# Chunk attention with a Mish FFN on Trainium2: softmax tiles transposed side by side, one more pair by DMA, q and k asked for earlier

## The chip, the cores and the metric

One core of one Trainium2 chip. The metric is the device time of one execution in microseconds; of several runs the median is taken. The kernel before takes 796.45 us (median of three runs, 796.07 to 797.13).

## What is computed

Attention within chunks of 64 tokens, then a feed-forward layer with the Mish function, all in float32:

```python
scores = scale * np.matmul(q_c, k_c.transpose(0, 1, 2, 4, 3))
scores = scores - np.max(scores, axis=-1, keepdims=True)
attn = np.exp(scores)
attn = attn / (np.sum(attn, axis=-1, keepdims=True) + 1e-09)
out = np.matmul(attn, v_c)
...
h = x @ w_in
sp = np.where(h > 20.0, h, np.log1p(np.exp(np.minimum(h, 20.0))))
g = h * np.tanh(sp)
return (g @ w_out).astype(np.float32)
```

q, k and v have 8 batches, 8 heads, 576 tokens and 64 columns; x has 4608 rows of 512, w_in is 512 by 2048, w_out 2048 by 512.

## The kernel before, in words

**Tiles and pairs.** The 4608 tokens are 36 tiles of 128; attention works on 18 pairs of tiles. The first eight tiles go through the FFN in a plain phase (lines L389 and L424), in which the attention of the first eight pairs (0 to 7) is done as well. The other 28 tiles form four blocks of 896 rows.

**The Strassen phase.** For the four blocks both FFN products are done by a Strassen scheme with seven products in place of eight. Each block has eight sets of 14 steps, 32 sets in all. An even step is one up product (`s_up`, L881, six matmuls into the banks `al`, `b` or `g`), an odd step one down product (`s_down`, L1000, six matmuls into a bank `d`, one of two that take turns). After a down product `s_out` brings the bank into `totals`, which lies in the room `sums`: by a copy on ACT (L1026) where a block's total is written for the first time, by an addition on DVE (L1028) otherwise. When a block is done, DVE transposes the totals (L1031), and `s_store` (L1044) writes half of them to the output by four DMAs of 224 KB. A block's first copy into a half of `sums` has to wait until the stores of the block before have read that half. The stores of the first block are at steps 137 and 141, those of the second at 249 and 253. The down products run 15 steps behind the up products, so the last eight or so of a block come in the next block's first sets.

**Pairs 8 to 17** are worked in beside the steps. `MEET` lists the steps at which the pairs meet: pair 8 has its scores at step 36 and its values at step 50, where the scores of pair 9 follow, and so on. `plan_pair` (L1235) puts each operation of a pair at a step: q and k are asked for 9 steps ahead of the scores (`p_load`, L707), v three steps after them (`load_v`, L246), then come max, subtraction (DVE), exponential (ACT), sum and normalisation (`p_norm`, L760, DVE). The normalised tile has to be transposed before the values are formed. Pairs with 14 or 19 steps between scores and values do that on the PE (`p_transpose`, L770, eight matmuls with the identity into `pt`, and two copies on ACT, L778). The pairs with 28 or 56 steps (pairs 10, 11, 13, 15, 16) do it by DMA: POOL splits the words of a tile into two halves of 16 bits (`p_split`, L787), a DMA on SyncE's queue transposes them (`p_turn`, L793), and POOL joins them (`p_join`, L799).

**Places.** Room `c` has three places of 2 KB per partition. Tiles 0 and 1 of a pair lie in places 0 and 1; tile 0 is split into place 2, transferred back into place 0 and joined into place 2. Tile 1 is split into place 0, so its split comes after tile 0's join, seven steps later. The room `x32` has 14 KB for the rows of the next block and 2 KB (`waits`, at 14 KB) in which one tile of pair 7 and one of pair 14 waits until `x_late` (L696, steps 44 and 240). q, k and v of the pairs share three buffers of the pool `at`, together with a sum `xs` at steps 98, 210 and 322.

**The order of the work** is written out by hand. In each step `s_set` issues the up or the down product (and with it the load of the next ring tile, L861, after every fourth up product, and of a wo tile, L866, after every second down product), then the PE's operations of the pairs, then `s_out`, then the list of operations that are due at this step. Each engine, and SyncE's queue of DMAs, works in that order; an instruction that waits holds those behind it on its engine. The ring loads (1024 KB) are issued two ring tiles ahead, the wo loads (512 KB) three products ahead.

Of the kernel before, what the change touches and what calls it, by code (L numbers as in the profile page):

```python
# [13 lines left out]
U16 = mybir.dt.uint16  # L14
# [4 lines left out]
P = 128  # L19
CHUNK = 64  # L20
# [5 lines left out]
def kernel(  # L26
# [19 lines left out]
    NF, _, DM = w_out.shape  # L46
# [11 lines left out]
    NG = H // 2  # L58
# [16 lines left out]
    KB = 1024  # L75
# [16 lines left out]
    def view(name, start, shape, dtype=F32):  # L92

        n = math.prod(shape)
        o = rooms[name]
        assert start % 4 == 0 and start // 4 + n <= o.shape[1]
        o = o[:, start // 4 : start // 4 + n]
        if dtype != F32:
            o = o.bitcast(dtype)
        if len(shape) > 1:  # L100
            names = "abcde"[: len(shape)]
            o = o.rearrange(
                f"p ({' '.join(names)}) -> p {' '.join(names)}", **dict(zip(names, shape))
            )
        return o
# [123 lines left out]
    st = {}  # L229
# [13 lines left out]
    def load_v(j, vs=None):  # L243
        if vs is None:
            vs = at.tile([P, 2, H, D], F32, name=f"v_{j}", tag="A")
        nc.sync.dma_start(out=vs, in_=v[2 * j : 2 * j + 2].rearrange("t p h c -> p t h c"))  # L246
        st[j]["v"] = vs
# [429 lines left out]
    x32 = []  # L677
# [20 lines left out]
    def a_x(j, t):  # L698
        x_put(2 * j + t, st[j]["av", 0][:, :, t])
# [4 lines left out]
    def p_load(j):  # L704
        qk = [at.tile([P, 2, H, CHUNK], F32, name=f"{n}_{j}", tag="A") for n in "qk"]
        for x, src in zip(qk, (q, k)):
            nc.sync.dma_start(out=x, in_=src[2 * j : 2 * j + 2].rearrange("t p h c -> p t h c"))  # L707
        st[j] = {"q": qk[0], "k": qk[1]}

    def p_scores(j, z):  # L710
        d = st[j]
        o = places["a", z - 1], places["b"]
        for c in range(2):
            d["s", c] = o[c].rearrange("p (t g k) -> p t g k", t=2, g=NG)
        for t in range(2):
            for g in range(NG):
                for h in range(2):
                    for c in range(2):
                        rows = slice(c * CHUNK, (c + 1) * CHUNK)
                        nc.tensor.matmul(  # L720
                            d["s", c][h * CHUNK : (h + 1) * CHUNK, t, g],
                            lhsT=d["q"][rows, t, 2 * g + h],
                            rhs=d["k"][rows, t, 2 * g + h],
                            start=True,
                            stop=True,
                        )

    def p_max(j, c):
        st[j]["m", c] = m = sm_p.tile([P, 2, NG], F32, name=f"m_{j}_{c}", tag="m")
        nc.vector.tensor_reduce(out=m, in_=st[j]["s", c], op=ALU.max, axis=AX.X)  # L730

    def p_sub(j, c):
        d = st[j]
        if c == 0:
            d["pp"] = view("c", 0, [2, NG, 2, CHUNK])
            for t in range(2):
                d["p", t] = d["pp"][:, t]
        nc.vector.tensor_tensor(
            out=d["pp"][:, :, :, c],
            in0=d["s", c],  # L740
            in1=d["m", c].unsqueeze(3).broadcast_to([P, 2, NG, CHUNK]),
            op=ALU.subtract,
        )

    def p_exp(j, t):
        p = st[j]["p", t]
        nc.scalar.activation(out=p, in_=p, func=AF.Exp, scale=SCALE)

    def p_sum(j, t):
        r = small(j, "r", slice(t, t + 1))  # L750
        nc.vector.tensor_reduce(
            out=r.rearrange("p c n -> p n c"), in_=st[j]["p", t], op=ALU.add, axis=AX.X
        )
        nc.vector.tensor_scalar(out=r, in0=r, scalar1=1e-9, scalar2=None, op0=ALU.add)
        nc.vector.reciprocal(out=r, in_=r)

    def p_norm(j, t):
        p = st[j]["p", t].rearrange("p g c k -> p c g k")
        r = st[j]["r", t]
        nc.vector.tensor_tensor(  # L760
            out=p, in0=p, in1=r.unsqueeze(3).broadcast_to([P, 2, NG, CHUNK]), op=ALU.mult
        )

    def p_transpose(j):
        d = st[j]
        pool, tag = home[0]
        d["pt"] = pool.tile([P, 2, NG, P], F32, name=f"pt_{j}", tag=tag)
        for t in range(2):
            for g in range(NG):
                nc.tensor.transpose(  # L770
                    out=d["pt"][:, t, g],
                    in_=d["p", t][:, g].rearrange("p c k -> p (c k)"),
                    identity=ident,
                )

    def p_copy(j, t):
        d = st[j]
        nc.scalar.copy(  # L778
            out=d["p", t].rearrange("p g c k -> p (g c k)"),
            in_=d["pt"][:, t].rearrange("p g n -> p (g n)"),  # L780
        )

    def half_words(slot):
        return view("c", 2 * KB * slot, [DM]).bitcast(U16)

    def p_split(j, t):
        nc.gpsimd.tensor_copy(  # L787
            out=half_words((2, 0)[t]).rearrange("p (b n) -> p b n", b=2),
            in_=half_words(t).rearrange("p (n b) -> p b n", b=2),
        )  # L790

    def p_turn(j, t):
        nc.sync.dma_start_transpose(  # L793
            out=half_words(t).rearrange("p (m n) -> p m n", n=P), in_=half_words((2, 0)[t])
        )

    def p_join(j, t):
        st[j]["p", t] = view("c", 2 * KB * (2, 0)[t], [NG, 2, CHUNK])
        nc.gpsimd.tensor_copy(  # L799
            out=half_words((2, 0)[t]).rearrange("p (n b) -> p b n", b=2),  # L800
            in_=half_words(t).rearrange("p (b n) -> p b n", b=2),
        )

    def p_values(j):
        d = st[j]
        o = banks(j, "av", BOTH, home[0])
        for t in range(2):
            ps = d["p", t].rearrange("p g c k -> p (g c) k").unsqueeze(1)
            small_mm(o[:, :, t : t + 1], d["v"][:, t : t + 1], ps, FIRST)
# [377 lines left out]
    def when(z, i, *ops):  # L1187
        due.setdefault((z, i), []).extend(ops)
# [37 lines left out]
        for k, m in (2, 0), (5, 3), (3, 4), (4, 7):  # L1226
            when(z, m, lambda k=k: x_sum(b, k))

    MEET = (36, 50, 64, 92, 148, 162, 190, 204, 260, 288, 307)
    NEAR = dict(exp=5, sum=(6, 7), norm=(7, 8), t=11)  # L1230
    MID = dict(exp=5, sum=(8, 9), norm=(10, 12), t=16)
    FAR = dict(exp=33, sum=(36, 37), norm=(38, 40), t=44)
    pe = {}

    def plan_pair(j, start, end):  # L1235

        n = NEAR if end - start < 16 else MID if end - start < 30 else FAR

        def at_(m, *ops):
            when(*divmod(m, STEPS), *ops)  # L1240

        def on_pe(m, op):
            pe.setdefault(divmod(m, STEPS), []).append(op)

        at_(8 if start == MEET[0] else start - 9, lambda: p_load(j))
        on_pe(start, lambda: p_scores(j, start // STEPS))
        at_(start + 3, lambda: load_v(j))
        for t in range(2):
            at_(start + 1 + 2 * t, lambda t=t: p_max(j, t))
            at_(start + 2 + 2 * t, lambda t=t: p_sub(j, t))  # L1250
            at_(start + n["exp"], lambda t=t: p_exp(j, t))
            at_(start + n["sum"][t], lambda t=t: p_sum(j, t))
            at_(start + n["norm"][t], lambda t=t: p_norm(j, t))
            if end - start < 28:
                at_(start + n["t"] + 1, lambda t=t: p_copy(j, t))
            else:
                m = start + n["norm"][0] + 7 * t
                at_(m + 1, lambda t=t: p_split(j, t))
                at_(m + 2, lambda t=t: p_turn(j, t))
                at_(m + 8, lambda t=t: p_join(j, t))  # L1260
            at_(end + 1, lambda t=t: a_x(j, t))
        if end - start < 28:
            on_pe(start + n["t"], lambda: p_transpose(j))
        on_pe(end, lambda: p_values(j))

# [20 lines left out]
    with tc.manual_schedule():  # L1286
# [38 lines left out]
        for n in "b", "g":  # L1325
            places[n] = ps_b.tile([P, DM], F32, name=n, tag=n)
        for j, pair in zip(range(AHEAD[-1] + 1, NPAIR), zip(MEET, MEET[1:])):
            plan_pair(j, *pair)
# [55 lines left out]
```

## Time and profile before

| what | value |
|---|---|
| median of 3 runs | 796.45 us |
| profiled execution | 795.96 us, span 794.1 us |
| PE busy | 781.3 us (98%) |
| DVE, ACT, POOL busy | 592.6, 475.9, 296.1 us |
| DMA | 204.95 MB, mean 258 GB/s |
| TensorE clock granted | 0.999 of full speed |

The span runs from the first to the last recorded instruction; the time has some 2 us around it. PE is TensorE's matmul, PEld its weight loads, DVE VectorE, ACT ScalarE, POOL GpSimd, SPq the queue of SyncE, from which nearly all DMAs are issued. In rows of the timeline and of the chain the first number is the start and the second the length, in microseconds; "[1.96 <-PE d L1000]" is the idle time of the engine just before and what ended it. "d<-u,wo" names the output and the inputs. Where an instruction waits for several things, the row names the one that came last by the profile.

### The profile page before, as it was taken

Reading aid. Unit: us, or ns where it says so; the run is one execution under the profiler, and the core shown is the slowest. Engines: PE = TensorE matmul, PEld = TensorE weight load, DVE = VectorE, ACT = ScalarE, POOL = GpSimd, SP = SyncE. Lnnn points to the kernel's source line nnn. Section 1 sums busy time; section 2 is a strip of 40 time slices with the busy share of each in tenths; the row PEclk is TensorE's granted clock in tenths of the full one; section 3 lists DMA queues with packets and bytes.
Section 4 is the critical chain, followed back from the end, with each engine's and each line's share of the span. In section 5 each row is a group of like instructions: output and inputs, shape, how many; then the busy total and the mean of one; then the engine's idle time right before and its main releaser. Section 6 shows DMA issues by size and latency. Waiting matters only on the chain.

```text
span 794.1 us, 15299 instructions
## 1 busy us (share of the span) xinstructions
PE 781.3 (98%) x5940; PEld 701.4 (88%) x5940; DVE 592.6 (75%) x929; ACT 475.9 (60%) x855; POOL 296.1 (37%) x259
## 2 busy tenths in 40 slices
PE   8999999999999999999999999999999999999996
PEld 7887888888889999999899999999999999999986
DVE  6897978888866776799577679977575897455666
ACT  5988865666676665555566466647465654644440
POOL 2000026556363235533434435454433452333340
PEclk9999999999999999999999999999999999999999
DMA  7798867989978777765987866689965667866537
GB/s 292 245 312 292 276 229 242 350 285 333 374 244 295 268 263 222 291 225 181 328 333 237 297 254 233 220 234 373 284 235 185 227 217 242 291 224 220 182 117 172
DMA packets 95112, 204.95 MB, mean 258 GB/s; under 512 B 24128, under 2 KB 47168, under 8 KB 87872
## 3 DMA queue, kind: packets, MB, share of 16 engines
q1 hardware_dynamic: 90752, 202.01, 74.9%
q10 hardware_dynamic: 4288, 1.97, 1.0%
q8 instruction: 47, 0.77, 0.4%
q14 instruction: 25, 0.20, 0.1%
HBM read 162.53 MB, written 38.80 MB: 254 GB/s over the span
## 4 chain that ended last, share of the span: by engine, by line
PE 75%; DVE 10%; ACT 6%; DMA 3%; issue 2%; POOL 1%; SPq 0%; DVEq 0%; POOLq 0%; ACTq 0%
PE d L1000 28%; PE al L881 16%; PE o_o L424 8%; PE g L881 8%; PE h L389 7%; PE b L881 4%; DMA k<-in_k 2%; PE av L256 2%; DVE sums L1028 1%; DVE sums L1031 1%; PE al L720 1%; DMA v<-in_v 1%; DVE c L192 1%; PE s L256 1%; DVE c L760 1%
## 5 line engine op out<-in xcount | busy, mean ns | idle before, releaser
L1000 PE MATMUL d<-u,wo 128*128 128x448 f32 x796 | 203.8, 363 | 0.0
L1028 DVE TENSOR_TENSOR sums<-d,sums 128x448 f32<-128x448 f32 x192 | 118.8, 619 | 78.4 <-PE d L1000 78.1
L881 PE MATMUL al<-xo,ring 128*128 128x448 f32 x768 | 174.6, 362 | 0.0
L1000 PEld LDWEIGHTS d<-u,wo 128*128 128x128 f32 x796 | 148.6, 187 | 11.7 <-DVE u L960 0.6
L881 PEld LDWEIGHTS al<-xo,ring 128*128 128x128 f32 x768 | 143.3, 187 | 11.0 <-ACT sums L926 0.5
L881 PE MATMUL g<-xo,ring 128*128 128x448 f32 x384 | 87.6, 363 | 0.2 <-ACT y L926 0.2
L881 PEld LDWEIGHTS g<-xo,ring 128*128 128x128 f32 x384 | 71.6, 187 | 5.4 <-ACT y L926 0.6
L1000 PE MATMUL d<-yr,wo 128*128 128x448 f32 x192 | 56.7, 363 | 0.0
L1000 PE MATMUL d<-xo,wo 128*128 128x448 f32 x182 | 54.9, 364 | 0.0
L1000 PE MATMUL d<-g,wo 128*128 128x448 f32 x174 | 51.9, 363 | 0.2 <-DVE sums L1028 0.2
L950 ACT ACTIVATE b<-b 128x448 f32<-128x448 f32 x32 | 16.9, 528 | 52.0 <-DVE b L936 51.9
L640 POOL TENSOR_TENSOR c<-c 128x256 f32<-128x256 f32 x12 | 10.8, 901 | 98.2 <-DVE c L608 96.2
L881 PE MATMUL b<-xo,ring 128*128 128x448 f32 x192 | 43.6, 362 | 0.0
L950 ACT ACTIVATE y<-y 128x448 f32<-128x448 f32 x22 | 12.7, 577 | 47.6 <-DVE y L936 47.6
L982 POOL TENSOR_TENSOR z<-y,z 128x448 f32<-128x448 f32 x24 | 27.8, 1157 | 35.8 <-DVE y L982 21.9
L424 PE MATMUL o_o<-xo,g 128*128 128x512 f32 x168 | 40.8, 392 | 0.1
L389 PE MATMUL h<-x,xo 128*128 128x512 f32 x168 | 40.9, 392 | 0.0
L950 ACT ACTIVATE z<-g 128x448 f32<-128x448 f32 x32 | 17.4, 544 | 39.0 <-DVE g L936 28.0
L1000 PEld LDWEIGHTS d<-yr,wo 128*128 128x128 f32 x192 | 36.0, 187 | 2.7 <-ACT sums L1026 0.3
L881 PEld LDWEIGHTS b<-xo,ring 128*128 128x128 f32 x192 | 36.0, 187 | 2.5
L424 PEld LDWEIGHTS o_o<-xo,g 128*128 128x128 f32 x168 | 31.2, 188 | 6.6 <-DVE g L411 0.2
L389 PEld LDWEIGHTS h<-x,xo 128*128 128x128 f32 x168 | 31.2, 188 | 6.5
(261 smaller groups left out, 1656.3 us busy)
## 6 DMA issues: line engine op xcount, KB each, us to landing
ring<-dwi SPq DMA_DIRECT2D x56, 1024.0 KB, 7.1
wo<-dwo SPq DMA_DIRECT2D x112, 512.0 KB, 4.5
sums<-in_w_in SPq DMA_DIRECT2D x16, 512.0 KB, 5.4
sums<-in_w_out SPq DMA_DIRECT2D x16, 512.0 KB, 5.6
q<-in_q SPq DMA_DIRECT2D x16, 512.0 KB, 6.4
k<-in_k SPq DMA_DIRECT2D x16, 512.0 KB, 6.9
v<-in_v SPq DMA_DIRECT2D x16, 512.0 KB, 6.3
dwo<-sums SPq DMA_DIRECT2D x15, 512.0 KB, 5.2
```

Of the source, the lines that this page charges most:

```text
L192: nc.vector.scalar_tensor_tensor(out=c, in0=c, scalar=3, in1=a[:, :, 0], op0=left, op1=either)
L256: nc.tensor.matmul(o[h * CHUNK : (h + 1) * CHUNK, c, t - ts.start, g], lhsT=l[rows, t, 2 * g + h], rhs=r[rows, t, 2 * g + h], start=True, ...
L389: nc.tensor.matmul(h[:, cols], lhsT=wi(f, w_, kt), rhs=x[:, kt, cols], start=(n == 0), stop=(n == 3 * NK - 1),)
L424: nc.tensor.matmul(acc[t], lhsT=g[:, sl], rhs=w_part(f, w_), start=(f == 0 and n == 0), stop=(f == NF - 1 and n == 2),)
L640: nc.gpsimd.tensor_tensor(out=o, in0=a, in1=b, op=op)
L720: nc.tensor.matmul(d["s", c][h * CHUNK : (h + 1) * CHUNK, t, g], lhsT=d["q"][rows, t, 2 * g + h], rhs=d["k"][rows, t, 2 * g + h], start=Tr ...
L760: nc.vector.tensor_tensor(out=p, in0=p, in1=r.unsqueeze(3).broadcast_to([P, 2, NG, CHUNK]), op=ALU.mult)
L881: nc.tensor.matmul(o[:, :HALF], lhsT=w_[:, wn, kt * P : (kt + 1) * P], rhs=x[:, xn, kt], start=(n == 0 and k < 3), stop=(n == 5), skip_gro ...
L950: nc.scalar.activation(out=take(z, 12) if n == 12 else i, in_=i, func=AF.Mish)
L982: engine.tensor_tensor(out=o, in0=l, in1=r, op=ALU.subtract)
L1000: nc.tensor.matmul(o[:, :HALF], lhsT=wos[(len(DOWN) * y + kk) % 4][:, i, part, h * P : (h + 1) * P], rhs=x, start=(m == 0 and k in (5, 2, 1)),
L1028: nc.vector.tensor_tensor(out=o, in0=i, in1=o, op=ALU.add)
```

## The change

Three things are altered.

1. A fourth place of 2 KB, the `waits` area of `x32`, joins the three of room `c`. Tile 0 is split into and joined in place 2 as before, tile 1 in place 3. Tile 1's split comes one step after its own normalisation, its transfer one step later, and both joins ten steps after the normalisation (tile 0's was eight). In a pair with 28 steps that puts the splits at steps 11 and 13, the transfers at 12 and 14 and the joins at 20 and 22 after the scores; before they were at 11 and 18, 12 and 19, 18 and 25. In a pair with 56 steps they move from 39, 40, 46 and 46, 47, 53 to 39, 40, 48 and 41, 42, 50.
2. The last pair (17) has its values at step 316, not 307. With 28 steps it is now one of the pairs that go by DMA, the sixth of ten.
3. q and k are asked for 12 steps ahead of the scores, not 9 (the first of the ten pairs, at step 8, is left as it is).

```diff
+    def p_place(n):
+        return ("c", 2 * KB * n) if n < 3 else ("x32", 14 * KB)
+
+    def half_words(n):
+        return view(*p_place(n), [DM]).bitcast(U16)
 
     def p_split(j, t):
         nc.gpsimd.tensor_copy(
-            out=half_words((2, 0)[t]).rearrange("p (b n) -> p b n", b=2),
+            out=half_words(t + 2).rearrange("p (b n) -> p b n", b=2),
             in_=half_words(t).rearrange("p (n b) -> p b n", b=2),
         )
 
     def p_turn(j, t):
         nc.sync.dma_start_transpose(
-            out=half_words(t).rearrange("p (m n) -> p m n", n=P), in_=half_words((2, 0)[t])
+            out=half_words(t).rearrange("p (m n) -> p m n", n=P), in_=half_words(t + 2)
         )
 
     def p_join(j, t):
-        st[j]["p", t] = view("c", 2 * KB * (2, 0)[t], [NG, 2, CHUNK])
+        st[j]["p", t] = view(*p_place(t + 2), [NG, 2, CHUNK])
         nc.gpsimd.tensor_copy(
-            out=half_words((2, 0)[t]).rearrange("p (n b) -> p b n", b=2),
+            out=half_words(t + 2).rearrange("p (n b) -> p b n", b=2),
             in_=half_words(t).rearrange("p (b n) -> p b n", b=2),
         )
...
-    MEET = (36, 50, 64, 92, 148, 162, 190, 204, 260, 288, 307)
+    MEET = (36, 50, 64, 92, 148, 162, 190, 204, 260, 288, 316)
     NEAR = dict(exp=5, sum=(6, 7), norm=(7, 8), t=11)
-    MID = dict(exp=5, sum=(8, 9), norm=(10, 12), t=16)
-    FAR = dict(exp=33, sum=(36, 37), norm=(38, 40), t=44)
+    MID = dict(exp=5, sum=(8, 9), norm=(10, 12))
+    FAR = dict(exp=33, sum=(36, 37), norm=(38, 40))
...
-        at_(8 if start == MEET[0] else start - 9, lambda: p_load(j))
+        at_(8 if start == MEET[0] else start - 12, lambda: p_load(j))
...
-            if end - start < 28:
+            if n is NEAR:
                 at_(start + n["t"] + 1, lambda t=t: p_copy(j, t))
             else:
-                m = start + n["norm"][0] + 7 * t
+                m = start + n["norm"][t]
                 at_(m + 1, lambda t=t: p_split(j, t))
                 at_(m + 2, lambda t=t: p_turn(j, t))
-                at_(m + 8, lambda t=t: p_join(j, t))
+                at_(m + 10, lambda t=t: p_join(j, t))
             at_(end + 1, lambda t=t: a_x(j, t))
-        if end - start < 28:
+        if n is NEAR:
             on_pe(start + n["t"], lambda: p_transpose(j))
         on_pe(end, lambda: p_values(j))
```

## Rows read from the trace of the kernel before

**Rows 1.** The page, busy us, share of the span and instructions by engine.
```profile
PE 781.3 (98%) x5940; PEld 701.4 (88%) x5940; DVE 592.6 (75%) x929; ACT 475.9 (60%) x855; POOL 296.1 (37%) x259
```

**Rows 2.** Waits of PE (columns: us in total, times, longest us).
```profile
PE al L720 <- DMA k<-in_k: 1.0, 2, 0.8
```

**Rows 3.** The chain that ended last around step 304 (start us, us, what).
```profile
594.04 1.20 PE g L881 x6
595.24 0.87 PE pt L770 x8
596.12 1.20 PE d L1000 x6
```

**Rows 4.** Timeline of ACT and of PE's weight loads at two block ends.
```profile
386.91 0.53 ACT L1026 COPY sums<-d 128x448 f32<-128x448 f32 x1 [1.96 <-PE d L1000]
387.74 0.19 PEld L1000 LDWEIGHTS d<-xo,wo 128*128 128x128 f32 x1
534.21 0.53 ACT L1026 COPY sums<-d 128x448 f32<-128x448 f32 x1 [2.47 <-DMA out<-sums]
534.80 0.19 PEld L1000 LDWEIGHTS d<-yr,wo 128*128 128x128 f32 x1 [0.28 <-ACT sums L1026]
```

**Rows 5.** Timeline of SyncE's queue at the two block ends.
```profile
379.92 3.53 SPq L1044 DMA_DIRECT2D out<-sums  x4
384.46 1.36 SPq L793 DMA_TRANSPOSE c<-c  x1
385.87 0.63 SPq L707 DMA_DIRECT2D q<-in_q  x1
526.71 3.65 SPq L1044 DMA_DIRECT2D out<-sums  x4
532.79 0.66 SPq L707 DMA_DIRECT2D q<-in_q  x1
```

**Rows 6.** Single DMA issues at the first block end, with their time to landing.
```profile
L866 SPq DMA_DIRECT2D wo<-dwo x1: 525/525/525, 375.6 to 375.6; - x1
DMA to landing us min/median/max: 3.8/3.8/3.8
L861 SPq DMA_DIRECT2D ring<-dwi x1: 423/423/423, 376.2 to 376.2; - x1
DMA to landing us min/median/max: 5.7/5.7/5.7
L866 SPq DMA_DIRECT2D wo<-dwo x1: 319/319/319, 377.3 to 377.3; - x1
DMA to landing us min/median/max: 5.9/5.9/5.9
L1044 SPq DMA_DIRECT2D out<-sums x1: 1804/1804/1804, 381.6 to 381.6; - x1
DMA to landing us min/median/max: 5.2/5.2/5.2
```

**Rows 7.** Stretches of 2 us: busy by engine, PEclk, DMA share, GB/s.
```profile
376.00:378.00 2.00, 2.00 (x12) 1.81 (x12) 1.97 (x4) 0.97 (x2) 0.00 (x0) 1.00 0.76 172
378.00:380.00 2.00, 2.00 (x12) 1.87 (x11) 1.97 (x5) 1.15 (x3) 1.16 (x1) 1.00 1.06 428
380.00:382.00 2.00, 2.00 (x12) 1.87 (x11) 1.97 (x4) 1.57 (x4) 1.52 (x2) 1.00 0.96 389
526.00:528.00 2.00, 2.00 (x12) 1.88 (x11) 1.93 (x5) 1.34 (x4) 0.93 (x2) 1.00 0.98 403
```

**Rows 8.** DVE's second norm of pair 11, POOL after it, splits and joins.
```profile
374.03 0.67 DVE L760 TENSOR_TENSOR c<-c,r 128x512 f32<-128x512 f32 x1
378.25 1.16 POOL L960 TENSOR_TENSOR u<-sums,yr 128x448 fp32r<-128x448 f32 x1 [4.77 <-ACT yr L954]
L787 POOL COPY c<-c x10: 1037/1040/1262, 301.2 to 564.8; 128x1024 uint16<-128x1024 uint16 x10
L799 POOL COPY c<-c x10: 1343/1352/1757, 310.0 to 569.9; 128x1024 uint16<-128x1024 uint16 x10
```

More of the change, by code (lines that the diff above doesn't have):

```diff
@@ L781, in p_copy @@
         )
-    def half_words(slot):
-        return view("c", 2 * KB * slot, [DM]).bitcast(U16)
+    def p_place(n):
+        return ("c", 2 * KB * n) if n < 3 else ("x32", 14 * KB)
+    def half_words(n):
+        return view(*p_place(n), [DM]).bitcast(U16)
     def p_split(j, t):
         nc.gpsimd.tensor_copy(
-            out=half_words((2, 0)[t]).rearrange("p (b n) -> p b n", b=2),
+            out=half_words(t + 2).rearrange("p (b n) -> p b n", b=2),
             in_=half_words(t).rearrange("p (n b) -> p b n", b=2),
```

## The prediction

> **What bounds the kernel now.** I read the page's busy times first, then the waits of the PE, then the chain that ended last, and only then the queue of SyncE around the places where the change moves something. The PE is busy for 98% of the span [rows 1]. So a microsecond counts only if it is PE work removed, PE idle time removed, or PE idle time added. In the Strassen phase a step (six matmuls) takes 1.20 us [rows 3]; all step numbers below are turned into time by that.
>
> The longest waits of the PE in this phase are two, both for a late k [rows 2]. They belong to pairs 12 and 16, whose scores are due at steps 148 and 260. SyncE shows why: q and k are planned for steps 139 and 251, and there they stand behind four output stores and a transfer by transposition, so they are issued only at 385.87 and 532.79 [rows 5].
>
> One more near-wait decides this case. Steps 137 and 249 each store half of a finished block (four DMAs of 224 KB from `sums`). The next block's first result is copied by ACT into the same half of `sums`, so that copy must wait until all four stores have read it. After the second block ACT sat idle for 2.47 us for those stores, and the PE's next `d` matmul began right when the copy was done [rows 4]. After the first block the last store lands at 381.6 + 5.2 = 386.8 [rows 6] and the copy starts at 386.91; the PE's weight load that needs the freed bank comes at 387.74, 0.3 us after the copy's end at 387.44 [rows 4]. So at both block ends the landing of the stores sets the PE, with 0.3 us to spare in the first and nothing in the second.
>
> **The change part by part.** *The last pair goes by transfer.* Eight transposes leave the PE: the chain shows 0.87 us for them between two full steps [rows 3], so −0.9. The values stand alone on the PE at step 316 as they did at 307, at the same price. Two ACT copies from PSUM go, two splits and two joins come on POOL: 2 × 1.04 + 2 × 1.35 = 4.8 us [rows 8], spread over 11 steps (13 us) on an engine that is 37% busy [rows 1]. I cost that at nothing; without the cover a late join would hold the values at step 316, one for one. Its two transposing DMAs and the later copies into x32 end at step 317, five steps (6 us) before the first reader at 322: nothing.
>
> *Both tiles beside each other.* Tile 1's split no longer waits for tile 0's join: split at norm + 1, transfer one step later. For pair 11 the second norm ends at 374.70 and POOL has nothing from 373.5 on [rows 8], so its split would end near 375.8 and its transfer would be issued right behind the ring load of 376.2 [rows 6], not at 384.46 [rows 5]. Joins now end six steps ahead of the values instead of three, and POOL's subtraction in step 13 no longer queues behind a join and a split. No PE wait of size hangs on either [rows 2]: nothing. If a late split held SyncE there, the loads behind it would wait; the first of them are the wo loads, which are issued three products (12 steps, 14 us) ahead of their use.
>
> *q and k 12 steps ahead.* Slots: three buffers; at steps 136 and 248 one holds v, two are free, so the loads need not wait. In the pairs 14 steps apart they now come one step before the previous pair's v, which has 11 steps (13 us) and so stays hidden. For pairs 12 and 16 k lands long before the scores: the waits of 0.8 and 0.2 go, −1.0 [rows 2].
>
> But what do they overtake? Step 136 and step 248 lie *before* the stores of 137 and 249. In before SyncE issued ring, wo, four stores, transfer, q, k; after, it issues ring, transfer, q, k, wo, four stores. All but the transfer run on the one queue of SyncE. The landings of this queue come in order of issue: wo of 375.6 at 379.4, ring of 376.2 at 381.9, wo of 377.3 at 383.2, last store at 386.8 [rows 6]. And the DMA engines are full in that stretch, with shares of 1.06 and 0.96 (0.98 after the second block) [rows 7]. So 1,049 KB in front push the stores back by the time these bytes take, called D. Nearest rows: the same 1,049 KB of the ring load added 381.9 − 379.4 = 2.5 us [rows 6]; at the 389 to 428 GB/s of this stretch [rows 7] it is 2.5 to 2.7. I take 2.6. Bounds: 0, if the stores are not held by what is in front; 5.7, the ring load's whole time from issue to landing [rows 6], if nothing overlaps. The transfer moving ahead could add up to a microsecond of sharing (hence 3.6 as a practical upper end).
>
> What the PE then loses: D − 0.3 = 2.3 at the first block end, D = 2.6 at the second, 4.9 together. Third block end: no pair is near it, unchanged.
>
> The Trainium skill (DMA: Bandwidth & Descriptors, "Where 436 GB/s comes from") puts loads from HBM at about 358 GB/s for one core; as an estimate from that page, 1,049 KB would take 2.9 us and the sum would be +3.6. The rows of this stretch show more than that, and they are used.
>
> *Sum:* −0.9 − 1.0 + 4.9 = **+3.0 us**. The profiled execution took 795.96 us (span 794.1); the median is 796.45, 0.49 above it. I put the sum on the median: 799.4.
>
> **The rivals.** *A, other side: the stores are not held.* Place: SyncE's queue at 380 and 527 us. If the stores' packets are served beside q and k, D is 0 and only the gains stay: 796.45 − 1.9 = 794.6, faster. It decides at D = 1.1, where 2D − 0.3 equals 1.9. For it: k arrives with time to spare in any case, and stores are small in bytes. Against it: the landings in issue order [rows 6] and full engines [rows 7].
>
> The Trainium skill (DMA: Bandwidth & Descriptors, "Queues, rings and completion order") says that data descriptors carry no barrier, a later one may finish before an earlier one, and completion is not first-in-first-out per issuing engine. By that rule this rival would hold; in the four landings of this case none overtook another, so I give it 0.26 and not more.
>
> *B: D is about half,* since q and k are issued at some 378 to 379 and part of them flows before the stores are ready at 379.92 [rows 5], or because the stores' own four transfers, and not the bytes in front, set their landing. D near 1.1 gives 2.2 − 0.3 − 1.9 = 0: 796.5, within 0.2%. For it: the DMA moved only 172 GB/s in 376 to 378 [rows 7]. Against: that is before q and k can be issued. Chance 0.19.
>
> *C: POOL becomes the limit in the last pair,* a late join holding the values: at most the 1.76 us that a join took beside other work [rows 8], 1.8 − 1.9 and no stores held: also near 796.4. Small, inside B's chance.
>
> **How the numbers follow.** 0.2% of 796.45 is 1.6 us, about what a measurement here can tell from no change. Slower by more needs D above 1.9; faster by more needs D below about 0.3. Forecast (D from 1.9 up): 0.55, at 799.4, its own range 798.0 to 801.5 (D 1.9 to 3.6). B: 0.19. A: 0.26. The range has to reach A, so 794.4 to 801.2; left out are the fast tail of A (gains over 2.1, perhaps 0.1) and D over 3.5 (0.07).
>
> **What would show it.** In the profile of after: no `pt` matmuls from pair 17 (32 instead of 40 of that line) and a step 304 without the 0.87 gap; no wait of the PE for k; q and k issued near 378 and 525 ahead of four stores. Right, if the `d` line shows PE idle of over 2 us near 388 and 535 behind ACT's copy into `sums`, itself waiting for the stores, and these land near 389.4 and 536.7. Wrong, if the copy starts near 387 and 534 as before: then the time is near 794.6 and the failed step is D. New waits of the PE for a join on POOL would make C right.

## The result and the profile after

The changed kernel takes 804.02 us (median of 4 runs, 802.31 to 804.64) against 796.26 us for the kernel before in the same comparison; the ratio is 1.0097, with a 95% interval of 1.0073 to 1.0122. It is slower, as forecast, but by 7.8 us where 3.0 were forecast, and 804.02 lies outside the range. The profiled execution has a span of 802.8 us, 8.7 more than before.

The page's busy line of after, which answers to [rows 1]:

```profile
PE 783.5 (98%) x5932; PEld 703.7 (88%) x5932; DVE 590.4 (74%) x929; ACT 474.6 (59%) x853; POOL 303.3 (38%) x263
```

The PE's busy time hardly moves. The list of its waits on other engines (columns: us in total, times, longest us) has no k any more [rows 2], and a new first line:

```profile
PE d L1003 <- ACT sums L1029: 7.1, 2, 3.6
```

Lines have moved by three: L1026 is L1029 now, L1044 is L1047, L1000 is L1003. The timelines of ACT and of the PE at both block ends, to be held against [rows 4]:

```profile
390.85 0.53 ACT L1029 COPY sums<-d 128x448 f32<-128x448 f32 x1 [6.15 <-DMA out<-sums]
542.59 0.53 ACT L1029 COPY sums<-d 128x448 f32<-128x448 f32 x1 [6.33 <-DMA out<-sums]
```

```profile
386.49 1.36 PE L884 MATMUL g<-xo,ring 128*128 128x448 f32 x6
391.44 0.74 PE L1003 MATMUL d<-xo,wo 128*128 128x448 f32 x1 [3.58 <-ACT sums L1029]
...
399.76 1.36 PE L884 MATMUL g<-xo,ring 128*128 128x448 f32 x6
...
538.28 1.36 PE L884 MATMUL g<-xo,ring 128*128 128x448 f32 x6
543.17 0.47 PE L1003 MATMUL d<-yr,wo 128*128 128x448 f32 x1 [3.53 <-ACT sums L1029]
...
550.68 1.36 PE L884 MATMUL g<-xo,ring 128*128 128x448 f32 x6
```

The same products in the kernel before:

```profile
386.74 1.36 PE L881 MATMUL g<-xo,ring 128*128 128x448 f32 x6
394.79 1.36 PE L881 MATMUL g<-xo,ring 128*128 128x448 f32 x6
533.53 1.36 PE L881 MATMUL g<-xo,ring 128*128 128x448 f32 x6
541.24 1.36 PE L881 MATMUL g<-xo,ring 128*128 128x448 f32 x6
```

From one `g` product to the next it is 399.76 − 386.49 = 13.27 us and 550.68 − 538.28 = 12.40 us. In the kernel before the same two stretches take 8.05 us and 7.71 us. So the block ends lose 5.2 + 4.7 = 9.9 us. Elsewhere the changed kernel gains 1.2 us: 0.25 ahead of the first block end, 0.2 between the two, and 0.7 after the second, where the eight transposes are gone. What is left is the 8.7 us of the span.

Why the copy is late stands in SyncE's queue and in the landings. The row with `c<-x` is the transposing DMA of tile 1, called the second transfer below; that of tile 0, the first transfer, is issued at 373.26, ahead of the rows shown. The issues at the first block end, against [rows 5]:

```profile
376.59 1.77 SPq L796 DMA_TRANSPOSE c<-x  x1
378.41 0.62 SPq L707 DMA_DIRECT2D q<-in_q  x1
379.08 0.57 SPq L707 DMA_DIRECT2D k<-in_k  x1
379.75 0.64 SPq L869 DMA_DIRECT2D wo<-dwo  x1
380.49 4.02 SPq L1047 DMA_DIRECT2D out<-sums  x4
```

Two single issues with their time to landing, against [rows 6]:

```profile
L707 SPq DMA_DIRECT2D k<-in_k x1: 571/571/571, 379.1 to 379.1; - x1
DMA to landing us min/median/max: 7.2/7.2/7.2
L1047 SPq DMA_DIRECT2D out<-sums x1: 1458/1458/1458, 383.1 to 383.1; - x1
DMA to landing us min/median/max: 7.6/7.6/7.6
```

k lands at 379.1 + 7.2 = 386.3, the last store at 383.1 + 7.6 = 390.7, and the copy starts at 390.85. Before, the last store landed at 386.8. The transfers share the queue of the other DMAs, as the page's section on queues shows: the changed kernel has two more transfers of 256 KB, and they are added to q1 (packets, MB, share; first before, then after):

```profile
q1 hardware_dynamic: 90752, 202.01, 74.9%
q1 hardware_dynamic: 92864, 202.53, 75.5%
```

And there is a second loss, which the waits don't list. Stretches of 2 us (columns as in [rows 7]):

```profile
386.00:388.00 2.00, 1.85 (x10) 1.40 (x8) 0.00 (x0) 0.00 (x0) 0.55 (x1) 1.00 1.07 368
388.00:390.00 2.00, 0.00 (x0) 0.00 (x0) 0.00 (x0) 0.00 (x0) 0.00 (x0) 0.98 1.35 312
390.00:392.00 2.00, 0.56 (x2) 0.52 (x3) 0.00 (x0) 1.15 (x3) 0.07 (x1) 0.50 0.78 265
392.00:394.00 2.00, 2.00 (x7) 1.78 (x6) 0.00 (x0) 2.00 (x6) 1.07 (x1) 0.50 1.13 336
394.00:396.00 2.00, 2.00 (x7) 1.50 (x5) 1.16 (x2) 0.92 (x3) 0.00 (x0) 0.50 1.04 299
396.00:398.00 2.00, 2.00 (x105) 1.79 (x108) 0.63 (x1) 0.58 (x1) 0.00 (x0) 0.82 0.94 369
398.00:400.00 2.00, 2.00 (x44) 1.84 (x37) 0.97 (x2) 0.04 (x1) 0.00 (x0) 1.00 0.49 203
...
544.00:546.00 2.00, 2.00 (x7) 1.79 (x6) 0.19 (x1) 2.00 (x6) 0.80 (x1) 0.50 1.21 262
```

After the PE has stood idle for 3.6 us the granted clock is 0.50, the lower level of 1.2 GHz; between 392 and 396 the PE starts 7 matmuls in 2 us, where it starts 12 at 1.00 [rows 7]. From 398 on it is back at 1.00. The last row shows the same behind the second block end.

### The profile page after: what moved, and what is told of

It is laid out like the page before. It is cut to its first block, busy times and chain, and to the rows that moved or that the text cites. A ratio compares the mean times of both kernels' runs of the same rounds, so it can differ in the third digit from the quotient of the medians.

```text
span 802.8 us, 15296 instructions
## 1 busy us (share of the span) xinstructions
PE 783.5 (98%) x5932; PEld 703.7 (88%) x5932; DVE 590.4 (74%) x929; ACT 474.6 (59%) x853; POOL 303.3 (38%) x263
## 4 chain that ended last, share of the span: by engine, by line
PE 77%; DVE 8%; ACT 7%; DMA 5%; issue 2%; SPq 1%; ACTq 0%; DVEq 0%
PE d L1003 29%; PE al L884 17%; PE g L884 8%; PE o_o L424 8%; PE h L389 7%; PE b L884 4%; DMA out<-sums 2%; PE av L256 2%; DMA sums<-in_w_out 2%; DVE sums L1031 1%; DVE sums L1034 1%; ACT c L170 1%; PE al L720 1%; ACT sums L179 1%; DMA sums<-in_w_in 1%
## 5 line engine op out<-in xcount | busy, mean ns | idle before, releaser
L1003 PE MATMUL d<-u,wo 128*128 128x448 f32 x796 | 204.4, 364 | 0.0
L1003 PEld LDWEIGHTS d<-u,wo 128*128 128x128 f32 x796 | 149.1, 188 | 11.5 <-DVE u L963 0.6
L884 PEld LDWEIGHTS al<-xo,ring 128*128 128x128 f32 x768 | 145.2, 190 | 11.0 <-ACT sums L929 0.3
L1003 PE MATMUL d<-yr,wo 128*128 128x448 f32 x192 | 56.7, 363 | 3.5 <-ACT sums L1029 3.5
L1003 PE MATMUL d<-xo,wo 128*128 128x448 f32 x182 | 56.3, 372 | 3.6 <-ACT sums L1029 3.6
L1003 PE MATMUL d<-g,wo 128*128 128x448 f32 x174 | 52.0, 364 | 0.2 <-DVE sums L1031 0.2
L1003 PEld LDWEIGHTS d<-yr,wo 128*128 128x128 f32 x192 | 36.0, 188 | 6.3 <-ACT sums L1029 3.9
L1003 PEld LDWEIGHTS d<-xo,wo 128*128 128x128 f32 x182 | 34.8, 192 | 6.5 <-ACT sums L1029 4.0
```

Source lines behind the costliest of these rows:

```text
L884: nc.tensor.matmul(o[:, :HALF], lhsT=w_[:, wn, kt * P : (kt + 1) * P], rhs=x[:, xn, kt], start=(n == 0 and k < 3), stop=(n == 5), skip_gro ...
L1003: nc.tensor.matmul(o[:, :HALF], lhsT=wos[(len(DOWN) * y + kk) % 4][:, i, part, h * P : (h + 1) * P], rhs=x, start=(m == 0 and k in (5, 2, 1)),
```

## The experiments

The theory was: q and k, and perhaps the second transfer, are in front of the stores; the stores hold ACT's copy, that the PE's `d` bank; and the idle PE loses its clock. The rivals were the second transfer alone, full DMA engines whatever the order, and, for the slow stretch behind the wait, anything but the clock.

**q and k behind the stores.** One step is enough to put them there.

```diff
-        at_(8 if start == MEET[0] else start - 12, lambda: p_load(j))
+        at_(8 if start == MEET[0] else start - 11, lambda: p_load(j))
```

> The changed kernel with q and k asked for 11 steps ahead, so that they are issued behind the four stores of steps 137 and 249 and no longer before them; all else as changed. Theory (q and k delay the stores in SyncE's queue, the stores delay ACT's copy, that the PE): the two PE waits of 3.6 and 3.5 us shrink to under 1 us each, the granted clock stays at 1.00 there, the last store lands near 387.5 in place of 390.7, time 794 to 796. Rival 1 (the second transfer and its split, moved ahead of the stores, do it): the waits stay near 3.5 us, time 803 to 804. Rival 2 (the DMA engines are simply full at the block end, whatever the order): the waits stay over 2 us, time 800 to 803.

795.26 us, ratio 1.0004 (0.9993 to 1.0014) to the kernel before. SyncE's queue, and the PE's wait:

```profile
379.63 4.42 SPq L1047 DMA_DIRECT2D out<-sums  x4
384.10 0.85 SPq L707 DMA_DIRECT2D q<-in_q  x1
```

```profile
PE d L1003 <- ACT sums L1029: 1.1, 2, 0.7
```

The whole loss is gone with one step's difference in the order of issue, and the granted clock stays at 1.00 at both block ends. What is left are two waits of 0.4 and 0.7 us, which eat the gain of the last pair. The second transfer alone, with q and k behind the stores, does not make the loss, and neither do full DMA engines whatever the order: both rivals of this run fall.

With 9 steps, the edit `start - 12` to `start - 9`:

> The changed kernel with q and k asked for 9 steps ahead as in the kernel before; the places, the transfers and the last pair as changed. Theory: like the run with 11 steps, 794 to 796, no PE wait for k since the second transfer no longer stands between the stores and q, k. Rival 1 (transfers and splits): 803 to 804. If k is late again, PE waits of about 1 us in total for it and 795 to 797.

795.72 us, ratio 0.9998 (0.9989 to 1.0008). The scores of pairs 12 and 16 do not wait for k, as the second transfer is no longer between the stores and q. The list still has a PE wait of 0.5 us behind the stores at the second block end; at the first `d` starts 0.3 us late. So the other two parts of the change together, the side-by-side places and the last pair, are worth nothing that can be measured.

**q and k alone.** The kernel before with only this:

```diff
-        at_(8 if start == MEET[0] else start - 9, lambda: p_load(j))
+        at_(8 if start == MEET[0] else start - 12, lambda: p_load(j))
```

> The kernel before with only the 12 steps ahead for q and k; places, transfers and the last pair as before. Theory: the stores come behind q and k, and the two PE waits appear, here without the second transfer in front: 2.5 to 3.5 us each, the granted clock falls to about a half behind them, time 800 to 804. Rival 1 (the second transfer is what holds the stores): no waits over 0.5 us, time 795 to 796.

800.44 us, ratio 1.0065 (1.0046 to 1.0084). The PE's wait for the copy and ACT's for the stores:

```profile
PE d L1000 <- ACT sums L1026: 4.2, 2, 2.2
```

```profile
ACT sums L1026 <- DMA out<-sums: 9.4, 2, 4.8
```

The waits are 2.0 and 2.2 us, a little under what was expected and far under the 3.6 and 3.5 of the whole change. So q and k do most of it, but not all. The granted clock falls to 0.50 here too, in 390 to 392 us. The `g` products and ACT's copies at the two block ends, for the measure used further down:

```profile
385.84 1.36 PE L881 MATMUL g<-xo,ring 128*128 128x448 f32 x6
388.66 0.53 ACT L1026 COPY sums<-d 128x448 f32<-128x448 f32 x1 [4.61 <-DMA out<-sums]
535.50 1.36 PE L881 MATMUL g<-xo,ring 128*128 128x448 f32 x6
538.46 0.53 ACT L1026 COPY sums<-d 128x448 f32<-128x448 f32 x1 [4.75 <-DMA out<-sums]
```

**Another queue for the stores.**

```diff
-            queue = nc.scalar if b == NSB - 1 and a % 2 else nc.sync
+            queue = nc.scalar if b < NSB - 1 or a % 2 else nc.sync
```

> The changed kernel with q and k 12 steps ahead, but with all stores of finished blocks issued from ACT's queue instead of SyncE's. Theory in its narrow form (it is the order within SyncE's queue): the stores are served beside q and k, the last lands within 6 us of its issue, the PE waits shrink below 1.5 us, time 794 to 798. Rival 2 (the DMA engines are full, order does not matter): the stores land as late as in the changed kernel, waits stay over 3 us, time 802 to 805. ACT spends some 2 to 4 us on issuing four stores at each half block, which may cost the PE up to 1 us each.

813.07 us, ratio 1.0218 (1.0201 to 1.0235): worse than either theory said. ACT's timeline, and the landings of the first four stores:

```profile
379.34 5.54 ACTq L1047 DMA_DIRECT2D out<-sums  x4
384.93 0.53 ACT L953 ACTIVATE al<-al 128x448 f32<-128x448 f32 x1 [6.18 <-DMA q<-in_q]
```

```profile
L1047 ACTq DMA_DIRECT2D out<-sums x4: 322/340/754, 379.3 to 384.6; - x4
DMA to landing us min/median/max: 7.9/9.7/12.3
```

The four issues held ACT for 5.5 us, and the stores landed 7.9 to 12.3 us after their issue, later than in SyncE's queue (7.5 to 7.9 at this block end of the changed kernel). So the narrow theory, that only the order within one queue matters, falls: on a queue of their own the stores were not served sooner. Whether what was issued before them held them, or the wo and ring loads that SyncE issued beside them (from 379.25 and at 383.16), this run does not separate. The time itself tests nothing here, as the PE also waits 3.3 and 3.2 us for results of DVE that come late in this run.

**The clock behind the wait.** Fillers after the up products of steps 146 and 258 keep the PE at work in the wait. They add matmuls into a bank that nobody reads.

```diff
+    def fill():
+        o = home[0][0].tile([P, 2, NG, P], F32, name="fill", tag=home[0][1])
+        for _ in range(30):
+            nc.tensor.matmul(o[:, 0, 0], lhsT=ident, rhs=ident, start=True, stop=True)
+
+    for m in 146, 258:
+        pe.setdefault(divmod(m, STEPS), []).append(fill)
```

> The changed kernel with 30 matmuls of the identity with itself, into a bank that nobody reads, after the up products of steps 146 and 258, where the PE waits 3.6 and 3.5 us (at the 0.11 us of a transpose they take 3.3 us). Clock theory (about 4 us of the loss is the lower granted clock behind the two waits): the granted clock stays at 1.00 at both places, the stretch from the first late d matmul to the next g product falls from 8.3 and 7.5 us to about 6, time 799 to 801. Rival (the slow matmuls behind the wait are slow because ACT and the DMA are late, not for the clock): no change, 803 to 805.

806.77 us, outside both expectations: each filler runs as two matmuls, 60 in the trace, and takes 6.6 us, longer than the wait. But behind it the first `d` at 393.81 and the next `g` at 399.72 are 5.91 us apart where the changed kernel takes 8.32 (391.44 to 399.76), at a granted clock of 1.00. The same with 15 fillers, so that they fit into the wait:

> The changed kernel with 15 instead of 30 fillers before each of the two late products (30 took 6.6 us, so 15 take 3.3, about the wait of 3.6 and 3.5). Clock theory: the granted clock stays at 1.00, the stretches behind the waits stay near 5.9 us, and since the fillers now fit into the wait the time falls by about 4 us against the changed kernel, to 799 to 801. Rival (the fillers cost as much as the clock gives back): 803 to 805.

800.47 us, ratio 1.0055 (1.0037 to 1.0072). That is 3.55 us less than the changed kernel by the medians, and 3.3 us by the ratios to the kernel before, each taken in its own comparison. Timeline and stretches of 2 us:

```profile
387.77 3.51 PE L1274 MATMUL fill<-ident 128*128 128x128 f32 x30
391.04 0.45 PE L1003 MATMUL d<-xo,wo 128*128 128x448 f32 x1
...
397.03 1.36 PE L884 MATMUL g<-xo,ring 128*128 128x448 f32 x6
...
540.39 0.47 PE L1003 MATMUL d<-yr,wo 128*128 128x448 f32 x1
...
546.45 1.36 PE L884 MATMUL g<-xo,ring 128*128 128x448 f32 x6
```

```profile
390.00:392.00 2.00, 2.00 (x17) 1.95 (x16) 0.00 (x0) 1.62 (x4) 0.55 (x1) 1.00 0.80 283
392.00:394.00 2.00, 2.00 (x28) 1.47 (x30) 0.39 (x1) 2.00 (x6) 0.61 (x1) 1.00 1.13 337
```

The product starts nearly as late as in the changed kernel (4.47 and 4.84 us after `g` against 4.95 and 4.89), ACT is about as late and the DMA as full; but the clock stays at 1.00, and the stretch takes 5.99 us, in the second block 6.06 (540.39 to 546.45). Against 8.32 and 7.51 (543.17 to 550.68) the lower clock costs 2.3 + 1.45 = 3.8 us, close to what the time gives back.

**The last pair alone.** The kernel before with 316 in place of 307.

> The kernel before with only the last meeting step moved from 307 to 316: pair 17 goes by transfer in the places of before, q and k 9 steps ahead. Theory: the 0.87 us of the eight transposes leave the PE and nothing else moves, 0.5 to 1.2 us faster than before. Rival (the values at step 316 or the extra work on POOL hold the PE): same or up to 1 us slower.

794.77 us, ratio 0.998 (0.997 to 0.999). Faster by 0.8 to 2.4 us, with the 0.87 us of the transposes inside. The rival of this run falls.

**The pairs of 56 steps earlier.** `FAR = dict(exp=19, sum=(22, 23), norm=(24, 26))`, and q and k of pairs 12 and 16 26 steps ahead in the first kernel, 12 in the second. In both, tile 1 of pair 15 is split into the place in which pair 14's tile still waits (step 231, `x_late` is at 240), so one tile's rows of the result come from other data; all work is done, and the times are those of the full work.

> The changed kernel with the pairs of 56 steps (11 and 15) worked 14 steps earlier, from the exponential to the transfers, and q and k of pairs 12 and 16 asked for 26 steps ahead, so that neither transfers nor q and k are in front of the stores. Theory: no PE wait for the stores over 0.3 us, none for k, the transposes gone: 793 to 794.5, faster than both kernels. Rival (the stores are late at a block end whatever precedes them): waits of 0.5 us or more remain, 795 to 797.

> The changed kernel with the pairs of 56 steps worked 14 steps earlier, but q and k still 12 steps ahead, so that only q and k are in front of the stores and no transfer. Theory (both add up): PE waits of 2 to 2.3 us each as with the 12 steps alone, not 3.6, time 798 to 800. Rival (the transfer adds nothing, the rest is chance): waits of 3.3 us or more, 802 to 804.

799.85 us (ratio 1.0048, 1.0033 to 1.0064) and 802.27 us (1.0082, 1.0056 to 1.0109). Both missed: the first lies outside both of its expectations, the second within its rival's 802 to 804, but without the waits of 3.3 us that this rival needs. In the first the waits at the block ends are gone, yet new ones come at 14 steps earlier, here between 230 and 380 us:

```profile
PE al L884 <- ACT sums L929: 1.9, 1, 1.9
PE d L1003 <- DVE sums L1031: 1.0, 1, 1.0
```

The shift puts the pair's exponentials, sums and norms into the first steps of a block, where ACT and DVE cut the new block's x. ACT has its exponentials just ahead of the copy for which the first of these waits: that copy starts at 351.50 here and at 349.33 in the changed kernel. In the second the waits behind the stores are 0.4 and 1.7 us. They are short because with no transfer in front the stores land earlier, and not because q and k hold them less: ACT's copy starts 1.15 and 2.43 us after `g` here, and in the first kernel, with q and k gone from the front as well, 0.84 and 0.48 us before it. That puts the delay by q and k at 1.99 and 2.91 us. The shifted steps make the time of this kernel no clean measure.

**Apart.** The changed kernel with tile 1 of the 56-step pairs at its old steps, behind the stores, and q and k of pairs 12 and 16 well before them:

```diff
-        at_(8 if start == MEET[0] else start - 12, lambda: p_load(j))
+        at_(8 if start == MEET[0] else start - (26 if start in (148, 260) else 12), lambda: p_load(j))
...
-                m = start + n["norm"][t]
+                m = start + n["norm"][t] + (5 * t if n is FAR else 0)
...
-                at_(m + 10, lambda t=t: p_join(j, t))
+                at_(m + (8 if n is FAR and t else 10), lambda t=t: p_join(j, t))
```

> The changed kernel, with tile 1 of the two pairs of 56 steps split at 46, transferred at 47 and joined at 53 steps as before the change, so that it comes behind the stores, and with q and k of pairs 12 and 16 asked for 26 steps ahead, well before the stores; the other pairs side by side and 12 steps ahead as changed. Theory: with neither the second transfer nor q and k in front of the stores the PE waits fall to 0.3 us or less as before, k is never late, the transposes are gone: 793.5 to 795, faster than before by 0.2% or more. Rival (side by side in the pairs of 28 steps, or earlier q and k there, cost something of their own): 795.5 to 797.

794.00 us, ratio 0.9975 (0.9965 to 0.9986): faster than both kernels. The weight loads wait 0.3 us for the copy at each block end and never for k. And without the side-by-side places, only 316 and the 26 steps in the kernel before:

> The kernel before with the last pair at 316 and q and k of pairs 12 and 16 asked for 26 steps ahead; all places as before. Theory: the gain of the last pair and that of a k in time add up, 793.5 to 794.8 where the run with the last pair alone gave 794.8. Rival (k is on time by chance already when the last pair is moved): no better than that run, 794.5 to 795.5.

793.94 us, ratio 0.9979 (0.9967 to 0.9991): the same. It cannot be told from the run with the last pair alone (0.998) either, so that the gain of an early k adds up was not shown.

## Why the prediction was right and wrong

A measure for D that needs no common zero of the runs: how long after the start of the `g` product ACT's copy starts, at the first and second block end.

| kernel | in front of the stores | copy after `g`, us |
|---|---|---|
| 14 steps earlier, q and k 26 steps ahead | none of these | −0.84, −0.48 |
| 14 steps earlier, q and k 12 steps ahead | q, k | 1.15, 2.43 |
| before | first transfer | 0.17, 0.68 |
| 9 steps | both transfers | 0.92, 1.31 |
| only 12 steps | first transfer, q, k | 2.82, 2.96 |
| changed | both transfers, q, k | 4.36, 4.31 |

- *The last pair:* right; −0.9 forecast, −0.8 to −2.4 measured.
- *q and k overtake the stores, and these hold the PE:* right in place and cause. D of q and k alone is 2.82 − 0.17 = 2.65 and 2.96 − 0.68 = 2.28 us beside the first transfer, and 1.99 and 2.91 us with no transfer in front; forecast were 2.6. The four values scatter by 0.9 us, so that one end agrees to 0.05 us is luck; their mean of 2.46 is not far off. k's waits went, as forecast.
- *"The transfer moving ahead could add up to a microsecond of sharing (hence 3.6 as a practical upper end)":* this term failed first. It stood only in the upper bound; in the sum the second transfer cost nothing, as did both tiles side by side. With q and k in front, it adds 1.54 and 1.35 us to D, and D is 4.2 and 3.6 us; with q and k behind the stores it adds 0.75 and 0.63. The premise was *"All but the transfer run on the one queue of SyncE"*, and it is wrong: the transfers' packets are on q1 too, and the second transfer (issued at 376.59, landed at 383.6) stood in line in front of q. At the first block end part of the 1.54 us is SyncE's own time: the first store is issued 6.00 us before `g` (380.49), where it is 6.83 with only the 12 steps (379.01). At the second both have 6.8 us, and the transfer still adds 1.35.
- *"What the PE then loses: D − 0.3 = 2.3 at the first block end, D = 2.6 at the second, 4.9 together":* the start of `d` is 3.75 us late at the first end (391.44, due at 386.49 + 1.20) and 3.69 at the second (543.17, due at 538.28 + 1.20), 7.4 together. And idle time was counted one for one: *"So a microsecond counts only if it is PE work removed, PE idle time removed, or PE idle time added"* leaves out PE work that becomes slower. The lower clock behind the idle time, 3.8 us, was missing from the sum. This is the larger error; the other is 7.4 − 4.9 = 2.5 us.
- *Rival A* (stores not held) fell: the run with 11 steps shows that the order of issue decides. *Rival B* (half of D) fell by the measured D of 4.2 and 3.6 us. *Rival C* (a late join): the list of the PE's waits names none.

The sum with measured terms: −0.9 for the transposes, +7.4 + 3.8 at the block ends, less 1.3 us that before lost there itself (8.05 and 7.71 against 1.20 + 5.99 and 1.20 + 6.06), is +9.0; the span says +8.7.

Rival A leaned on the Trainium skill (DMA: Bandwidth & Descriptors, "Queues, rings and completion order"), which says that a later data descriptor may finish its write before an earlier one. The same sentence of the Trainium skill also says that each DMA engine consumes descriptors in ring order, so it gave the rival less ground than I took from it. Here the second transfer landed at 383.6, q at 385.0, k at 386.3, wo at 387.6 and the last store at 390.7, in the order of issue, and the stores came behind all that was in front.

## What to carry to other kernels

When a load is asked for earlier, look at which stores it passes in the issue order and who waits for those stores: here one step, 12 instead of 11, was worth 8.8 us by the medians and 7.4 us by the ratios to the kernel before. A wait of an otherwise full TensorE costs more than its length where the granted clock falls behind it, so price the work behind the wait at the lower clock too; here that was 3.8 us on top of 7.4. A prefetch that is late in two places can be moved in these two places alone: that cost nothing here (ratios 0.9975 and 0.9979), though a gain of its own was not shown.

## What the runs showed that was not expected

- A transfer by transposition of 256 KB put in front of q, k and the stores, delayed the stores by 1.35 to 1.54 us more, over half of what q and k with four times its bytes did in the same comparison (2.3 to 2.65). Why so few bytes cost so much stays open, beyond the 0.8 us of SyncE's own time at the first block end.
- Stores on a queue of their own, ACT's, were not served sooner: 7.9 to 12.3 us to landing against 7.5 to 7.9 at the first block end, and ACT was held 5.5 us by four issues.
- Matmuls that compute nothing of use, put into a wait, made the changed kernel 3.3 to 3.55 us faster, because the granted clock stayed at 1.00 behind it.
- The length of a wait alone did not tell whether the clock falls. Behind 2.04 us (only 12 steps) it fell to 0.50, behind 3.3 us in the run with ACT's queue it stayed at 1.00 (386 to 390 us), and behind 3.2 us in the same run it was 0.56 (542 to 544 us).
